# Sorting v of batch 0 from its rows as loaded, and score products behind 128 stationary columns

## The chip, the cores and the metric

The kernel runs on one core of one Trainium2 chip. Its time is the device time of one execution in microseconds, the median of three runs. Beside these runs stands one execution recorded by the hardware profiler; the profile's numbers come from that one. Engines are named as in the profile: PE is the matrix engine's multiplications, PEld its loads of stationary operands, DVE the vector engine, ACT the scalar engine, POOL the third elementwise engine, which also issues most loads from HBM, and SP the queue that issues the rest and the transposing DMAs.

## What is computed

Four batches of eight heads with 768 tokens of 64 elements go through an attention within blocks of 96 tokens, whose keys and values are first mixed between blocks by an 8 by 8 matrix P for each batch and head. Then come two layers of a feed-forward network on all 3072 tokens.

```python
P = sort_net
for _ in range(5):
    P = exp(P - max(P, -1));  P = P / (sum(P, -1) + 1e-9);  P = P / (sum(P, -2) + 1e-9)
k_sorted = einsum('bhij,bhjcd->bhicd', P, k_b)      # k_b: (4, 8, 8 blocks, 96, 64)
v_sorted = einsum('bhij,bhjcd->bhicd', P, v_b)
scores = matmul(q_b, k_sorted^T) / 8                # within a block: 96 x 96
attn = softmax(scores);  x = matmul(attn, v_sorted)
h = x @ w_in                                        # (3072, 512) @ (512, 2048)
out = (max(h, 0) + alpha * min(h, 0)) @ w_out       # (3072, 2048) @ (2048, 512)
```

Inputs and outputs are FP32; the loads turn q, k, v and the weights into BF16.

## The kernel before

The program is first written as a graph of operations (`G.add`: engine, function, estimated duration, the keys that it reads and writes). A table of numbers, `SEQ`, then lists all operations in one order; `arrange` takes each engine's own order from it, and `emit` writes that out with the semaphores that the keys call for. A number in the table is an operation's place in the graph; a letter behind it picks an engine where several may do it. An entry that begins with `i` is a filler: it puts so many matmuls of the identity (`warm`, L1042) into PE's stream, whose results nobody reads. So nothing is scheduled by due times: every engine works through a list that is fixed, and waits where a semaphore says so.

The work is done in 32 groups; group g is block g % 8 of batch g // 8, for all eight heads. `attention(g)` emits for a group:

- `s1` (L752 for batches 1 to 3, L755 for batch 0): eight products of q and sorted k, one for each head, 96 by 96 each, into the two banks of psS (psH for group 1). q is stationary, 96 columns, and k moves. In batch 0 a head uses 64 of the 128 rows of PE, so that two heads can lie on PE at a time.
- the maximum (L761, DVE) over each row of the scores.
- In batch 0 also `s2`: the same products turned (L776: k stationary, `nk` = 112 columns, of which 96 are read later, q moving), and onto them the negated maxima (L767: a stationary operand that repeats one column of `nm` 112 times, and the identity moving). Then one exponent for all heads (L799, ACT) writes ET.
- In the other batches the exponent (L788, ACT) takes the maximum as its bias, and a DMA transposes the result into ET.
- the product with sorted v (L808), its division by the sums (L816, L821), and the transposed copy into xT, directly or by a DMA.

The feed-forward network runs between these steps: `ffn1` (L870, PE; L880, ACT; L884, DVE) and `ffn2` (L910).

v is sorted ahead of its batch in eight units of eight elements of a head each (`prep_v`). For batches 1 to 3 POOL first spreads v into VDz, and PE sorts from there (L709). For batch 0 the rows of v are loaded as they are into VST: a partition holds 48 tokens of 64 elements, `3072` numbers. `conv_v(0, u)` then copies, on POOL, ACT or DVE as the table says, eight elements of all 48 tokens into a corner of the tile hT that is not otherwise in use yet: for each element 48 numbers side by side, and behind them 16 zeros, which one memset on POOL (L480) has written before. `prep_v(0, u)` (L714) takes each of these runs of 64 as a stationary operand, twice, for the upper and the lower 64 partitions of the output, with every second column of the matrix BDK moving. The copies out of PSUM into VS (line L401, where all plain copies have their line) drop nothing but order: v of a block comes to lie with 112 rows, 48 and 48 with zeros between.

```python
o = AP(hT, 8 * u * 64, [[HR, 128], [64, 8], [1, 48]])
i = AP(VST[0], 8 * u, [[3072, 128], [1, 8], [64, 48]])
```

In these access patterns each pair is a step and a count, in elements, the first pair being the partitions; the third number ahead of them is the offset.

Of the kernel before, what the change touches and what calls it, by code (L numbers as in the profile page):

```python
# [7 lines left out]
AP = bass.AP  # L8
ACTF = mybir.ActivationFunctionType
BF16 = mybir.dt.bfloat16  # L10
F32 = mybir.dt.float32
# [22 lines left out]
55 143 56 57 58 26 59 127 60 61 62 21 63 64 126 65 66 22 67 128 68 69 29 70 71 16 72 73 13 74 129 85 86 87 75  # L34
76 77 78 40 79 80 81 37 88 134 82 96 97d 94 91 92 98 38 89 130 12 144 95 90d i2Y 140 93a 83 84 100 i3Y 99d 20
136 101d 102d 105a 103d 154 i3Y 104 106 155 109 114 115 15 145 146 110 111 107d 112 113 i3Y 116 117d 147 108a
118 119d 148 122 123d 137 120 156 121 124 139 132 19 125d 135 233 133 157 i2Y 158 159 149 150 160d i3G 179 180
i1P 41 138 i2P 161 162d 151 152 18 181 30 35 36 34 153d 163 188 182 196 164 165 205 166 167p 197 189 190 191
232 206 183 230 184 207 192 193 185d 198 209 142 199 186 i1Y 231 237 210 141 194 195 221 208 131 187 213 200
211 212 222 244 214 201 223 215 216 248 245 224 249 202d 246 247 203 204d 250 251 217 225 258 218 236 226 262  # L40
263 219 220 234 241 235 227d 266 267 259 260 173 228 229 252 238 276 268 239 253 264 242 269 305 172 288d 170
174 240 280 261 279 286 243 270 315 265 289 290 277 278 271 287 293 294 306 307 272d 273 308 275 291 274 281
292 297 295 342 282d 298 283 309 284 296 301 302 285 316 343 317 310 299 344 300 328 311d 303 304 312 314 313d
320 326 332 32 321d 345 346 327 169p 333 324 329 347 325 353 348d 254 171p 349 334 335 175 354 255 256 350d
323 367 318 395 330 382 331 396 319d 392 336 351 393 383 384 397 394 419 416 420 322 352d 355 356 358d 31 365
398 399 337 366 357 338 408 421 409 359 257 425 417 400 418 426 422 339 428 360d 361 427 423 424 411 449 410
385 340 368 446 429 362 363 439 450 451 455 430 364d 447 448 369 176 458 459 414 443 456 415 386 387 388d 412
452 453 370 454 440 389 401 460 371 438 390d 402 476 488 457 479 413 403 404d 489 405 372 512 177 469 431 406d
432 477 178 441 461 480 444 478 482 442 481 485 433 434d 490 524 491 373 483 472 435 378 377 486 374 436 487
513 380 445 462 375 484 509 463 510 464d 470 379 471 506 507 381 511 465 466d 508 525 514 376 521 522 523 518  # L50
519 520 515 516d 526 527 492 517 474 545 475d 542 168 554 560 391 493 543 546 544 547 468 500 501 494d 555 548
473 561 549 550 502 437 495 496d 562 407 503d 551 552 556 499 577 553 563 578 579 498 504 505 533 528 529 557
558 589 530d 535 534 538 539 571 572 590 583 584 580 341 531 581 625 626 537 536 569 582 586 591 540 587 585
622 570d 541 573 574 575 532 600 576 627 588 623 631 598 624 599 564 632 559 628 629 565 601 634 566d 567 635
602 592 630 603 633 568d 637 636 655 638 639 608 604 605 593 594 595d 610 649 650 640 652 596 653 656 657 609
597 641 642 651 654 664 665 666 661 662 663 606 667 607 658 611 659 687 688 612 668 613 643 684 696 685 660
669 689 686 697 690 691 676 677 682 711 467 680 702 693 694 703 704 683d 695 678 698 692 699 679 713 714 644
645 497 700 670 705 722 723 731 732 810 712 719 720 751 681 733 734 717 817 744 752 646d 812 715 721 724 671
672 725 745 816 718 766 673d 728 767 742 753 726 727 647 729 730 674 706 748 701 757 707 768 618 769 743d 754
708d 758 759 749 750 801 802 755 756 716 746 763 764 747 735 736 760 737d 761 803 765 740 709 762 741 621 789  # L60
777 790 783 784 619 776 786 787 778d 813 785 779 788 836 837 791 792 780 793 775 781 738 804 795 796 782d 811
798 799 797 838 615 814 815d 620 830 770 614 617 818 819 844 845 800 616 771 821 772d 864 831 846 848 874 839
820 648 822 824 823 773 827 805 806 825 794 849 826 832 833 828 807d 829 808 847 872 852 875 865 675 855 873d
834 853 835 850 883 851 854 866 840 841 867 710 876 842d 843 774 877 884 856 857 858 878 879 885 886 898 899
887 859 861 860 912 913 862 880 863 868 869 870d 900 889 924 944 881 882 890 892 891 893 895 925 945 896 894
914 906 926 907 897 908 909 950 910 911 871 946 901 951 927 918 919 920 921 922 923 952 902 903 904d 915 739
932 933 934 935 936 947 948 928 953 970 937 938 939 905 941 942 916d 981 917 982 971 972 943 961 940 958 809
959 973 996 929 1010 930d 931 954 962 997 998 983 960 964 965 963 967 968 1022 955 956d 966 984 969 957 949
999 985 978 979 1023 987 988 980 1042 989 974 975 990 993 1043 1024 1048 976d 994 1044 995 991 992 1004 1005
1049 1007 1008 1050 1011 1012 977 1009 1019 1006 1016 1020 1021 1000 1017 1068 1001 1013 1018 1033 888 1014d  # L70
1034 1030 1031 1079 1080 1069 1002d 1070 1025 1026 1035 1039 1051 1003 1032 1040 1036 1037 1081 1041 1059 1038
1060 1056 1027 1071 1028d 1045 1052 1061 1057 1058 1065 1046 1047 1062 1053 1054d 1066 1082 1067 1085 1063
1064 1086 1055 1087 1072 1076 1015 1073 1100 1074d 1075 1077 1078 1091 1092 1093 1101 1088 1102 1097 1083d
1089 1090 1098 1099 1029 1124 1094 1095 1125 1126 1096 1106 1109 1110 1111 1084 1103 1127 986 1115 1107 1108
1116 1112 1104d 1145 1117 1105 1113 1114 1121 1122 1118 1119 1123 1120 1146 1133 1134 1166 1130 1135 1131 1132
1147 1148 1149 1139 1140 1136 1184 1141 1137 1138 1185 1128d 1151 1142 1152 1143 1153 1172 1157 1144 1154 1155
1156 1186 1173 1158 1174 1159 1160 1161 1162 1150 1163 1164 1165 1167 1168 1169 1187 1129 1188 1170 1189 1175
1176d 1171 1177 1178 1179 1180 1181 1182 1183
# [231 lines left out]
def bass_sinkhorn_attn__then__act_prelu_kernel(  # L310
# [774 lines left out]
```

## Time and profile before

| | |
|---|---|
| time, median of three runs | 235.86 us (235.62 to 236.09) |
| span of the profiled execution | 235.0 us |
| PE busy | 226.5 us (96%) |
| PE's loads of stationary operands busy | 143.5 us (61%) |
| DVE, ACT, POOL busy | 167.1, 156.5, 103.0 us |
| first product of the feed-forward network (L870) | at 29.83 us |
| score products of batch 0 (L755) | 18.1 to 48.8 us |
| score products of the other batches (L752) | 56.0 to 185.9 us |
| units of v of batch 0 on PE (L714) | 19.2 to 24.5 us |

The profile's span runs from the first to the last instruction; what a run takes beyond it, 0.86 us by the median, lies around it. Starts of matmuls are recorded, their ends are modelled: one that takes 40 ns of PE is shown with some 200 ns. So what a block of matmuls costs is read from its start to the start of the next block.

### The profile page before, as it was taken

How to read it: one execution, taken by the hardware profiler on the slowest of the kernel's cores; microseconds unless marked ns; L12 is line 12 of the kernel's file. 1: busy time of each engine (PE TensorE's matmuls, PEld its weight loads, DVE VectorE, ACT ScalarE, POOL GpSimd, SP SyncE). 2: the span in 40 equal slices, each digit the busy share in tenths (PEclk: the TensorE clock that was granted, in tenths of full speed). 3: DMA queues.
4: the chain of work that ended last, by engine and by line, in shares of the span. 5: the costliest groups of instructions: out<-in, count | busy, mean ns of one | idle time of the engine just before them, and what ended most of it. 6: DMA issues, size and time to landing. Idle time of an engine off the chain costs nothing.

```text
span 235.0 us, 6277 instructions
## 1 busy us (share of the span) xinstructions
PE 226.5 (96%) x2528; PEld 143.5 (61%) x2556; DVE 167.1 (71%) x339; ACT 156.5 (67%) x417; POOL 103.0 (44%) x149
## 2 busy tenths in 40 slices
PE   6899999999999999999999999999999999999995
PEld 4366689795566666565566565556565555555653
DVE  5759799999879788576679767567786577544541
ACT  4367565989989778877888767767776665333431
POOL 7999139639249994873959954000000000000000
PEclk9979999999999999999999999999999999999999
DMA  5999999994997799869929995954545423410203
GB/s 71 216 210 193 218 203 183 188 175 75 216 203 115 106 130 187 210 91 228 197 45 152 160 106 137 169 100 78 131 87 138 63 52 106 125 44 1 93 0 134
DMA packets 73389, 31.36 MB, mean 133 GB/s; under 512 B 64512, under 2 KB 68368, under 8 KB 73360
## 3 DMA queue, kind: packets, MB, share of 16 engines
q0 software_dynamic: 24816, 13.63, 43.1%
q1 hardware_dynamic: 48544, 17.33, 36.8%
q8 instruction: 20, 0.33, 0.6%
q14 instruction: 9, 0.07, 0.1%
HBM read 27.28 MB, written 6.29 MB: 143 GB/s over the span
## 4 chain that ended last, share of the span: by engine, by line
PE 92%; DVE 4%; issue 1%; ACT 1%; POOL 1%; POOLq 0%
PE psH L870 35%; PE psYP L910 30%; PE psS L752 4%; PE psS L910 4%; PE psO L808 3%; PE psYP L709 2%; PE psYP L668 2%; PE psYP L1042 2%; PE psS L767 2%; PE psO L843 1%; PE psS L776 1%; PE psS L755 1%; PE psO L714 1%; PE psO L910 1%; PE psYP L870 1%
## 5 line engine op out<-in xcount | busy, mean ns | idle before, releaser
L884 DVE SCALAR_TENSOR_TENSOR hT<-t,omaT,psH 128x384 bf16<-128x384 f32 (+1 forms) x140 | 76.5, 569 | 37.6 <-ACT t L880 36.8
L870 PE MATMUL psH<-xT,w_in_bf 128*128 128x384 bf16 (+1 forms) x560 | 96.7, 310 | 0.6 <-DVE hT L884 0.6
L880 ACT ACTIVATE t<-psH 128x384 f32<-128x384 f32 x126 | 61.1, 494 | 44.4 <-PE psH L870 41.5
L910 PE MATMUL psYP<-w_out_bf,hT 128*128 128x512 bf16 x310 | 79.2, 379 | 1.4
L870 PEld LDWEIGHTS psH<-xT,w_in_bf 128*128 128x128 bf16 x560 | 50.1, 98 | 28.8 <-DVE hT L884 2.1
L910 PEld LDWEIGHTS psYP<-w_out_bf,hT 128*128 128x128 bf16 x336 | 30.8, 98 | 28.2 <-DVE hT L884 0.3
L788 ACT ACTIVATE Esb<-psS,nf 96x96 bf16<-96x96 f32 x192 | 46.3, 346 | 0.9 <-DVE nf L761 0.8
L401 POOL COPY VDz<-VST 64x384 bf16<-64x384 bf16 x40 | 34.6, 865 | 17.3 <-PE psH L870 7.8
L655 POOL COPY KSz<-KS 64x512 bf16<-64x512 bf16 x36 | 21.9, 609 | 17.8 <-DMA KS<-in_k_dram 8.2
L761 DVE TENSOR_REDUCE nf<-psS 96x8 f32<-96x768 f32 x24 | 22.8, 949 | 6.6 <-PE psS L752 6.3
L821 DVE TENSOR_TENSOR xq<-psO,rec 96x512 bf16<-96x512 f32 x30 | 20.5, 684 | 0.7
L431 POOL DMA_DIRECT2D QN<-in_q_dram x24 | 19.9, 846 | 0.7 <-POOL QN L491 0.6
L401 ACT ACTIVATE outstg<-psYP 128x512 f32<-128x512 f32 x15 | 9.0, 601 | 7.7 <-PE psYP L910 7.6
L752 PEld LDWEIGHTS psS<-KT,QTz 128*96 128x96 bf16 x192 | 11.9, 125 | 2.8 <-ACT KT L401 0.2
L808 PEld LDWEIGHTS psO<-VS,ET 112*128 112x128 bf16 x248 | 11.1, 98 | 3.9 <-ACT xT L401 0.2
L808 PE MATMUL psO<-VS,ET 112*128 112x65 bf16 x248 | 12.7, 194 | 0.0
L752 PE MATMUL psS<-KT,QTz 128*96 128x96 bf16 x192 | 12.6, 208 | 0.0
L1042 PE MATMUL psYP<-identb 128*128 128x512 bf16 x39 | 11.6, 436 | 0.8 <-ACT identb L401 0.8
L401 ACT ACTIVATE VS<-psYP 112x512 bf16<-112x512 f32 x16 | 11.0, 690 | 1.9 <-PE psYP L714 1.1
L709 PEld LDWEIGHTS psYP<-BDV,VDz 128*128 128x128 bf16 x192 | 8.4, 98 | 2.7
L401 ACT ACTIVATE KT<-psYP 128x512 bf16<-128x512 f32 x14 | 8.4, 600 | 2.2 <-PE psYP L668 2.1
L816 DVE RECIPROCAL rec<-psO 96x8 f32<-96x8 f32 x31 | 6.2, 200 | 4.8 <-PE psO L808 4.7
(140 smaller groups left out, 208.1 us busy)
## 6 DMA issues: line engine op xcount, KB each, us to landing
out_dram<-outstg SPq DMA_DIRECT2D x23, 256.0 KB, 2.5
KS<-in_k_dram POOLq DMA_DIRECT2D x3, 768.0 KB, 9.7
QN<-in_q_dram POOLq DMA_DIRECT2D x24, 96.0 KB, 4.8
w_in_bf<-in_moe_w_in_dram POOLq DMA_DIRECT2D x4, 512.0 KB, 16.9
w_out_bf<-in_moe_w_out_dram POOLq DMA_DIRECT2D x2, 1024.0 KB, 18.5
VST<-in_v_dram POOLq DMA_DIRECT2D x4, 384.0 KB, 10.6
hT<-in_q_dram POOLq DMA_DIRECT2D x1, 768.0 KB, 7.4
VST<-in_v_dram POOLq DMA_DIRECT2D x1, 768.0 KB, 12.9
```

Of the source, the lines that this page charges most:

```text
L401: return e.activation(o, i, ACTF.Copy) if e is nc.scalar else e.tensor_copy(o, i)
L431: G.add(POOL, lambda e, h=h: e.dma_start(AP(QN, h * 128 + (h // 4) * 64, [[6144, 128], [1024, 6], [1, 64]]), AP(q.tensor, b * HB + h * S * ...
L655: G.add(POOL, lambda e, hp=hp: e.tensor_copy(AP(KSz, hp * 64 * 3072 + u % 3 * 1024 + hp * 64, [[3072, 64], [128, 8], [1, 64]]), AP(KS[n], ...
L752: inst = e.matmul(o, AP(QTz[n], hp * 3072 + h4 * 768 + i * 96, [[6144, 128], [1, 96]]), AP(KT[n], (h4 * 8 + i) * bk, [[ld, 128], [64, 2], ...
L761: G.add(DVE, lambda e: e.tensor_reduce(AP(nx, 0, [[8, 96], [4, 2], [1, 4]]), AP(psX, 0, [[1024, 96], [512, 2], [96, 4], [1, 96]]), AxisLis ...
L788: inst = e.activation(AP(Esb[me], p * 128, [[1024, 96], [64, 2], [1, 48]]), AP(psX, (p // 4) * 512 + (p % 4) * 96, [[1024, 96], [48, 2], [ ...
L808: inst = e.matmul(AP(psZ, hp * 512 + h4 * 68, [[1024, 128], [1, 65]]), AP(ET[me] if far else ET[m], pos(h4, hp) * 96, [[800, nk], [1, 128] ...
L821: return e.tensor_tensor(out=AP(xq[me], 0, [[512, 96], [256, 2], [64, 4], [1, 64]]), in0=AP(psZ, 0, [[1024, 96], [512, 2], [68, 4], [1, 64]]),
L870: inst = e.matmul(AP(pt, poff + x * n, [[1024, 128], [1, n]]), AP(w_in_bf, kt * DFF + (ft + x) * 128, [[KT_TILES * DFF, 128], [1, 128]]), ...
L880: G.add(ACT, lambda e: e.activation(AP(t1[tb], 0, [[384, 128], [1, k * n]]), AP(pt, poff, [[1024, 128], [1, k * n]]), ACTF.Relu, scale=-1. ...
L884: G.add(DVE, lambda e, x=x: e.scalar_tensor_tensor(out=AP(hT, (ft + x) * RING + tok % RING, [[FT_TILES * RING, 128], [1, n]]), in0=AP(t1[t ...
L910: inst = e.matmul(AP(bank[0], bank[1], [[1024, 128], [1, n]]), AP(hT, ft * RING + tok % RING, [[FT_TILES * RING, 128], [1, 128]]), AP(w_ou ...
```

## The change

**v of batch 0.** `load_v(0)` loads the rows of v straight into hT, 3072 numbers in each partition, where VST was the target before. The memset on POOL zeroes the 1024 numbers behind them (L480 before, in one piece now). `conv_v` has no case for batch 0 any more, and its eight operations are gone. `prep_v(0, u)` takes as stationary operand every 64th number from element `8 * u + dd` on: 48 tokens of that element and 16 zeros. It waits for the load of v and for the memset.

**128 columns.** `s1` takes 128 columns of q, the 96 of its block and the 32 behind them; where these would reach beyond what is there, or to tokens that come later, it stays at 96 (`wide`). `s2` takes 128 columns of sorted k (112 for the last head pair of block 7), and the repeated column of maxima stands 128 times. The results land in rows 96 to 127 of the banks, which nothing reads.

```diff
     def load_v(b, prio):
         if b == 0:
-            load_kv(VST, v, "VST", d_v, 9, b, prio)
+            G.add(POOL, lambda e: e.dma_start(AP(hT, 0, [[HR, 128], [1, 3072]]), AP(v.tensor, 0, [[3072, 128], [1, 3072]])),
+                  load_us, w=[("VST", 0)], prio=prio, dma=(d_v[0], 0))
             return
...
-        G.add(POOL, lambda e: e.memset(AP(hT, 48, [[HR, 128], [64, 64], [1, 16]]), 0.0), 900,
+        hz = hT.bitcast(F32)
+        G.add(POOL, lambda e: e.memset(AP(hz, 1536, [[HR // 2, 128], [1, 512]]), 0.0), 500,
               w=["VD0"], prio=-95.5)
...
     def conv_v(b, u, prio):
         vst = [("VST", b % 2)] + [("VST", b % 2, x) for x in range(4)]
-        if b == 0:
-            o = AP(hT, 8 * u * 64, [[HR, 128], [64, 8], [1, 48]])
-            i = AP(VST[0], 8 * u, [[3072, 128], [1, 8], [64, 48]])
-            G.add(ANY, lambda e: copy(e, o, i), {"act": 858, "dve": 540, "pool": 860},
-                  r=vst, w=[("VD", u)], prio=prio)
-            return
...
                     inst = e.matmul(AP(t, th * 64 * row + off + dd * 64, [[row, 64], [1, 64]]),
-                                    AP(hT, (8 * u + dd) * 64, [[HR, 128], [1, 64]]),
+                                    AP(hT, 8 * u + dd, [[HR, 128], [64, 64]]),
                                     AP(BDK, th, [[512, 128], [2, 64]]))
...
-            G.add(PE, f, 374, r=[("VD", u), "VD0", ("BDK", 0)], w=keys, prio=prio)
+            G.add(PE, f, 374, r=[("VST", 0), "VD0", ("BDK", 0)], w=keys, prio=prio)
...
-        qt_keys = [("QTzt", n, t) for t in range(i * 96 // 128, (i * 96 + 95) // 128 + 1)] if far else \
+        def wide(h4, hp):
+            return 96 if far and i == 3 or i == 7 and h4 == 3 and (hp or not far) else 128
+
+        qt_keys = [("QTzt", n, t % 6) for t in range(i * 96 // 128, (i * 96 + wide(0, 0) - 1) // 128 + 1)] if far else \
...
-                    o = AP(psX, (p // 4) * 512 + (p % 4) * 96, [[1024, 96], [1, 96]])
+                    w = wide(h4, hp)
+                    o = AP(psX, (p // 4) * 512 + (p % 4) * 96, [[1024, w], [1, 96]])
                     if far:
-                        inst = e.matmul(o, AP(QTz[n], hp * 3072 + h4 * 768 + i * 96, [[6144, 128], [1, 96]]),
+                        inst = e.matmul(o, AP(QTz[n], hp * 3072 + h4 * 768 + i * 96, [[6144, 128], [1, w]]),
                                         AP(KT[n], (h4 * 8 + i) * bk, [[ld, 128], [64, 2], [1, 48]]))
                     else:
-                        inst = e.matmul(o, AP(QTz[n], hp * 64 * 6144 + h4 * 768 + i * 96, [[6144, 64], [1, 96]]),
+                        inst = e.matmul(o, AP(QTz[n], hp * 64 * 6144 + h4 * 768 + i * 96, [[6144, 64], [1, w]]),
                                         AP(KT[n], hp * 64 * ld + (h4 * 8 + i) * bk, [[ld, 64], [64, 2], [1, 48]]))
...
-            return e.matmul(AP(psX, (p // 4) * 512 + (p % 4) * 96, [[1024, nk], [1, 96]]),
-                            AP(nm[m], p, [[8, 96], [0, nk]]),
+            return e.matmul(AP(psX, (p // 4) * 512 + (p % 4) * 96, [[1024, 128], [1, 96]]),
+                            AP(nm[m], p, [[8, 96], [0, 128]]),
                             AP(identb, 0, [[128, 96], [1, 96]]), start=False, stop=stop, skip_group_check=True)
...
-                    e.matmul(AP(psX, (p // 4) * 512 + (p % 4) * 96, [[1024, nk], [1, 96]]),
-                             AP(KT[n], hp * 64 * ld + (h4 * 8 + i) * bk, [[ld, 64], [1, nk]]),
+                    w = nk if i == 7 and h4 == 3 else 128
+                    e.matmul(AP(psX, (p // 4) * 512 + (p % 4) * 96, [[1024, w], [1, 96]]),
+                             AP(KT[n], hp * 64 * ld + (h4 * 8 + i) * bk, [[ld, 64], [1, w]]),
                              AP(QTz[n], hp * 64 * 6144 + h4 * 768 + i * 96, [[6144, 64], [1, 96]]),
                              start=h4 == 0, stop=False, skip_group_check=True)
...
-    for u in range(8):
-        conv_v(0, u, -45.5)
```

In the table the eight numbers of the copies, 102 to 109, fall out, and every later number is smaller by eight:

```diff
-136 101d 102d 105a 103d 154 i3Y 104 106 155 109 114 115 15 145 146 110 111 107d 112 113 i3Y 116 117d 147 108a
+128 101d 146 i3Y 147 106 107 15 137 138 102 103 104 105 i3Y 108 109d 139 110 111d 140 114 115d 129 112 148 113
```

Apart from the copies the order of every engine is what it was. DVE's list before, from the last copy of sorted k out of PSUM to the factor omaT of the feed-forward network (VST is v as loaded, nm the negated maxima, VS the sorted v):

```order
L401 CAST KT<-psH 128x32x2x8 [waits s_pe]
L401 COPY hT<-VST 128x8x48 [waits d_v0]
L401 COPY hT<-VST 128x8x48
L761 TENSOR_REDUCE nm<-psH 96x8 [waits s_pe]
L761 TENSOR_REDUCE nm<-psS 96x8 [waits s_pe]
L401 COPY hT<-VST 128x8x48
L401 CAST VS<-psO 112x64x8 [waits s_pe] x4
L967 TENSOR_SCALAR omaT<-psYP 128x16 [waits s_pe]
```

and the same place now:

```order
L400 CAST KT<-psH 128x32x2x8 [waits s_pe]
L760 TENSOR_REDUCE nm<-psH 96x8 [waits s_pe]
L760 TENSOR_REDUCE nm<-psS 96x8 [waits s_pe]
L400 CAST VS<-psO 112x64x8 [waits s_pe] x4
L965 TENSOR_SCALAR omaT<-psYP 128x16 [waits s_pe]
```

The three copies have gone from among the maxima and the copies of sorted v; the rest follows in the same order.

PE's list before, from a filler behind the scores of group 1 to the first turned ones (L714 are the units of v, L1042 the fillers, each row with the semaphores that its first instruction waits for):

```order
L1042 MATMUL psYP<-identb 128x512 x3
L714 MATMUL psYP<-BDK,hT 64x64 [waits s_pool]
L714 MATMUL psYP<-BDK,hT 64x64 x15
L755 MATMUL psS<-KT,QTz 96x96 x8
L714 MATMUL psO<-BDK,hT 64x64 [waits s_dve]
L714 MATMUL psO<-BDK,hT 64x64 x15
L714 MATMUL psO<-BDK,hT 64x64 [waits s_dve]
L714 MATMUL psO<-BDK,hT 64x64 x15
L1042 MATMUL psYP<-identb 128x512 x3
L714 MATMUL psO<-BDK,hT 64x64 [waits s_act]
L714 MATMUL psO<-BDK,hT 64x64 x15
L776 MATMUL psS<-QTz,KT 112x96 [waits s_dve]
```

and now:

```order
L1040 MATMUL psYP<-identb 128x512 x3
L709 MATMUL psYP<-BDK,hT 64x64 [waits d_v0,s_pool]
L709 MATMUL psYP<-BDK,hT 64x64 x15
L754 MATMUL psS<-KT,QTz 128x96 x8
L709 MATMUL psO<-BDK,hT 64x64 x32
L1040 MATMUL psYP<-identb 128x512 x3
L709 MATMUL psO<-BDK,hT 64x64 [waits s_act]
L709 MATMUL psO<-BDK,hT 64x64 x15
L776 MATMUL psS<-QTz,KT 128x96 [waits s_dve]
```

No matmul has moved. The first unit of v waits for the load of v (d_v0) and for the memset on POOL, the next two for nothing; the stationary operands of the scores have 128 columns. The lines of before and of now stand against each other thus: L714 and L709, L709 (batches 1 to 3) and L704, L752 and L751, L755 and L754, L767 and L766, L1042 and L1040, L401 and L400.

More of the change, by code (lines that the diff above doesn't have):

```diff
@@ L38 @@
[L38 to L62, printed above, removed]
@@ new lines @@
+619 580 615 623 590 616 591 556 624 551 620 621 557 593 626 558d 559 627 594 584 622 595 625 560d 629 628 647
+630 631 600 596 597 585 586 587d 602 641 642 632 644 588 645 648 649 601 589 633 634 643 646 656 657 658 653
+654 655 598 659 599 650 603 651 679 680 604 660 605 635 676 688 677 652 661 681 678 689 682 683 668 669 674
+703 459 672 694 685 686 695 696 675d 687 670 690 684 691 671 705 706 636 637 489 692 662 697 714 715 723 724
+802 704 711 712 743 673 725 726 709 809 736 744 638d 804 707 713 716 663 664 717 737 808 710 758 665d 720 759
@@ new lines @@
+833 859 702 868 834d 835 766 869 876 848 849 850 870 871 877 878 890 891 879 851 853 852 904 905 854 872 855
+860 861 862d 892 881 916 936 873 874 882 884 883 885 887 917 937 888 886 906 898 918 899 889 900 901 942 902
+903 863 938 893 943 919 910 911 912 913 914 915 944 894 895 896d 907 731 924 925 926 927 928 939 940 920 945
+962 929 930 931 897 933 934 908d 973 909 974 963 964 935 953 932 950 801 951 965 988 921 1002 922d 923 946 954
+989 990 975 952 956 957 955 959 960 1014 947 948d 958 976 961 949 941 991 977 970 971 1015 979 980 972 1034
@@ new lines @@
+981 966 967 982 985 1035 1016 1040 968d 986 1036 987 983 984 996 997 1041 999 1000 1042 1003 1004 969 1001
+1011 998 1008 1012 1013 992 1009 1060 993 1005 1010 1025 880 1006d 1026 1022 1023 1071 1072 1061 994d 1062
+1017 1018 1027 1031 1043 995 1024 1032 1028 1029 1073 1033 1051 1030 1052 1048 1019 1063 1020d 1037 1044 1053
+1049 1050 1057 1038 1039 1054 1045 1046d 1058 1074 1059 1077 1055 1056 1078 1047 1079 1064 1068 1007 1065 1092
+1066d 1067 1069 1070 1083 1084 1085 1093 1080 1094 1089 1075d 1081 1082 1090 1091 1021 1116 1086 1087 1117
```

47 lines of the change are left out of this document (28 added, 19 removed).

## The prediction

> **What bounds the kernel now.** I read the page first, for the engines' shares and the chain that ended last.
>
> ```profile
> span 235.0 us, 6277 instructions
> PE 226.5 (96%) x2528; PEld 143.5 (61%) x2556; DVE 167.1 (71%) x339; ACT 156.5 (67%) x417; POOL 103.0 (44%) x149
> PE 92%; DVE 4%; issue 1%; ACT 1%; POOL 1%; POOLq 0%
> ```
>
> TensorE (PE) is busy for 96% of the span, and 92% of the chain that ended last is PE work. A nanosecond that PE gains or loses should therefore reach the end, unless another engine sets the pace in that stage. Next come the windows, by stage.
>
> ```profile
> core 0: us, PE busy (x) PEld busy (x) DVE busy (x) ACT busy (x) POOL busy (x), PEclk, DMA share, GB/s
> 20.00:30.00 10.00, 9.62 (x215) 6.84 (x212) 7.60 (x19) 7.02 (x17) 4.39 (x6) 1.00 1.12 216
> 30.00:55.00 25.00, 24.89 (x405) 21.16 (x406) 23.53 (x58) 19.29 (x36) 15.90 (x25) 1.00 1.42 175
> ```
>
> The stretch up to 30 us holds the sort of batch 0 and its first groups; 30 to 55 us the rest of batch 0. There DVE is busy for 23.5 of 25 us beside a full PE: there a shorter PE could run into DVE. The granted clock is 1.00 in both.
>
> The profiled execution spans 235.0 us; the three runs have a median of 235.86 us. The 0.86 us between them lies outside the span and I leave it as it is: sums are made on the span and added to the median. What the measurement can tell from no change is 0.2%, here 0.47 us.
>
> **Part one: 128 columns in place of 96 and 112.** No instruction is added; eight groups of batch 0 get wider L755, L776 and L767, 24 groups of the other batches wider L752. What a load costs by its width stands in the groups (mean ns after the busy time):
>
> ```profile
> L752 PEld LDWEIGHTS psS<-KT,QTz 128*96 128x96 bf16 x192 | 11.9, 125 | 2.8 <-ACT KT L401 0.2
> L843 PEld LDWEIGHTS psO<-identb,xq 96*128 96x128 bf16 x60 | 3.7, 97 | 1.1 <-DVE xq L821 0.3
> L714 PEld LDWEIGHTS psO<-BDK,hT 128*64 128x64 bf16 x96 | 1.8, 112 | 0.6 <-ACT VS L401 0.4
> ```
>
> A load of 64 columns takes 112 ns and one of 96 takes 125: it grows with the columns. At 128 columns it takes 97, less than at 64.
>
> What that is worth on PE must be read from starts, since ends are modelled. PE alone, a stretch of batch 0 and a group of batch 1, and then, by line, what one matmul lasts (least, median, most, in ns):
>
> ```profile
> 32.57 0.41 PE L776 MATMUL psS<-QTz,KT 64*112 64x96 bf16 x8
> 32.91 0.61 PE L767 MATMUL psS<-identb,nm 96*112 96x96 bf16 x8
> 33.36 0.83 PE L870 MATMUL psH<-xT,w_in_bf 128*128 128x192 bf16 x8
> 34.02 0.34 PE L843 MATMUL psO<-identb,xq 96*128 96x96 bf16 x4
> 34.19 0.38 PE L1042 MATMUL psYP<-identb 128*128 128x512 bf16 x1
> 34.50 0.38 PE L755 MATMUL psS<-KT,QTz 64*96 64x96 bf16 x8
> 34.81 0.83 PE L870 MATMUL psH<-xT,w_in_bf 128*128 128x192 bf16 x8
> ...
> 56.11 0.52 PE L752 MATMUL psS<-KT,QTz 128*96 128x96 bf16 x8
> 56.47 0.81 PE L870 MATMUL psH<-xT,w_in_bf 128*128 128x384 bf16 x4
> ...
> L776 PE MATMUL psS<-QTz,KT x56: 212/212/247, 21.6 to 50.7; 64*112 64x96 bf16 x56
> L755 PE MATMUL psS<-KT,QTz x56: 205/205/240, 19.6 to 48.8; 64*96 64x96 bf16 x56
> ```
>
> L767: eight in 33.36 - 32.91 = 0.45 us, 56 ns each. L843 has the same 96 moving columns behind 128 stationary ones: four in 0.17 us, 43 ns each. So L767 falls to about 8 x 44 = 0.35, a gain of 0.10 us a group.
> L776 works in pairs on the two halves of the rows; its eight take 0.34 us. One matmul lasts 0.212, so starts are (0.41 - 0.212)/7 = 28 ns apart, 57 a pair; a pair can't go below the 44 of one moving operand, so 22 each: 7 x 6 = 0.04 us a group.
> L755, likewise: (0.38 - 0.205)/7 = 25, to 22: 0.02 us a group.
> L752: eight in 0.36 us, 45 ns each, which is what L843 takes with a fast load. The moving operand sets it, and the load lies beneath it. Gain: nothing, in 24 groups.
> Sum: 8 x (0.10 + 0.04 + 0.02) = 1.3 us at most. Bounds: if loads of half the rows stay slow at 128 columns, L776 gets 16 columns dearer (as from L755 to L776, 3 ns each) and L755 twice that, some 0.6 us in all, and 0.2 us is left of L767's 0.8. And where DVE sets the pace from 30 us on, only the three groups before it count: 0.5 us. [...]
> I take 0.9, between 0.5 and 1.3: PE and the chain of score, maximum, exponent through the banks psS both get shorter, but DVE has only 1.5 us free there.
>
> **Part two: v of batch 0 as loaded.** Eight copies go: three on POOL, three on DVE, two on ACT. What stood behind them, in order of time:
>
> ```profile
> 17.09 3.24 POOL L401 COPY hT<-VST 128x384 bf16<-128x384 bf16 x3
> ...
> 17.98 1.62 DVE L401 COPY hT<-VST 128x384 bf16<-128x384 bf16 x2
> 19.52 0.94 DVE L761 TENSOR_REDUCE nm<-psH 96x8 bf16<-96x768 f32 x1
> ...
> 21.61 0.28 PEld L776 LDWEIGHTS psS<-QTz,KT 64*112 64x112 bf16 x8
> ...
> 32.95 0.61 POOL L655 COPY KSz<-KS 64x512 bf16<-64x512 bf16 x1 [8.21 <-DMA KS<-in_k_dram]
> ```
>
> The first maximum, and the one behind it, can start 1 us earlier, but L776, which reads them, stands in PE's order behind four of the v units and a filler, and PE reaches it at 21.6 either way. On POOL the q loads of batch 1 are issued some 3 us earlier, and then POOL waits 8.2 us for k of batch 1, as before: nothing moves behind 32.95. The first v unit now waits for the DMA of v itself; POOL's first copy of it ran at 17.1, two us before PE gets there. PE's own waits here are few:
>
> ```profile
> PEld psO L714 <- ACT VS L401: 0.4, 1, 0.4
> PEld psYP L808 <- DVE omaT L967: 0.7, 1, 0.7
> ```
>
> The first is for a bank to be emptied and mostly lies under a filler of L1042; the second is behind the last v unit, whose copy out stays. So the copies' going is worth 0.1 us at most. They hid behind PE's fillers; I book nothing.
>
> The added cost is in the loads. The same 128 matmuls (L714) take 64 columns that lay side by side; now each column lies 128 bytes behind the last. The trace has no load with such a step. PE's pace there (its blocks in order of time, what one of L714 lasts, and a piece of the chain of waits for scale), and what such a step costs the three engines that made the copies, with a like one in order beside each:
>
> ```profile
> 19.86 0.69 PE L714 MATMUL psO<-BDK,hT 128*64 128x64 bf16 x32
> 20.49 0.82 PE L1042 MATMUL psYP<-identb 128*128 128x512 bf16 x3
> ...
> 29.83 0.83 PE L870 MATMUL psH<-xT,w_in_bf 128*128 128x192 bf16 x8
> ...
> L714 PE MATMUL psO<-BDK,hT x96: 192/196/217, 19.9 to 24.5; 128*64 128x64 bf16 x96
> ...
> 54.76 0.86 PE psYP L910 x4
> ...
> L401 DVE COPY hT<-VST x3: 508/598/1187, 18.0 to 21.3; 128x384 bf16<-128x384 bf16 x3
> L401 ACT ACTIVATE hT<-VST x2: 853/855/857, 17.7 to 21.4; 128x384 bf16<-128x384 bf16 x2
> ...
> L401 DVE COPY xT<-psO 128x384 bf16<-128x384 bf16 x9 | 3.2, 353 | 0.5 <-PE psO L843 0.4
> L880 ACT ACTIVATE t<-psH 128x384 f32<-128x384 f32 x126 | 61.1, 494 | 44.4 <-PE psH L870 41.5 <-DVE hT L884 1.8
> L401 POOL COPY VDz<-VST 64x384 bf16<-64x384 bf16 x40 | 34.6, 865 | 17.3 <-PE psH L870 7.8 <-PE psYP L709 5.6 <-DMA VST<-in_v_dram 1.9
> L655 POOL COPY KSz<-KS 64x512 bf16<-64x512 bf16 x36 | 21.9, 609 | 17.8 <-DMA KS<-in_k_dram 8.2 <-PE psYP L668 7.7
> ```
>
> Thirty-two L714 take 0.63 us, 20 ns each with the block's start, starts (0.69 - 0.196)/31 = 16 apart inside. A column of a moving operand takes 0.42 ns (L910's four of 512 in 0.86 us), so 64 take 27: the two halves of the output run side by side, and a load has some 32 ns before it is late. It has no slack to lose more than a few ns in.
> The step's price per element: ACT (855 - 494)/384 = 0.94 ns, POOL 865/384 - 609/512 = 1.06 ns, DVE at its best (508 - 353)/384 = 0.40 ns. The least it can be is 0. For 64 columns: 0, 26 (DVE) or 60 ns (ACT) a load; with two halves side by side 0, 13 or 30 ns a matmul; times 128: 0, 1.65 or 3.85 us, on PE, in a stage without slack, ahead of all the rest. If the halves' loads queue, the last two double.
> I take DVE's, 1.65 us: PE's column of 0.42 ns is nearest to DVE's pace, and 0.40 more makes one column in two clocks of it.
> [...]
>
> **Sum.** 235.86 + 1.65 - 0.9 = 236.6 us. Its own range: 235.86 + 1.65 - 1.3 = 236.2, up to 237.5 with half of ACT's excess.
>
> **The rivals.**
> *Loads with a step cost PE nothing.* Then part one is all: 235.86 - 0.9 = 235.0, from 234.6 to 235.4. For it: a copy made to put columns side by side may have been made only for the 16 zero columns at the end of each 64. Against: ACT, POOL and DVE all pay. It decides if L714's starts stay 16 ns apart. Chance 0.32.
> *They cost what ACT pays.* 235.86 + 3.85 - 0.9 = 238.8, from 237.5 up to 242.7 where the two halves' loads also queue. For it: two engines of three agree at about 1 ns. [...] Chance 0.22.
> *Little of either.* The step is free or cheap, and DVE at 94% eats what PE gains after 30 us: within 0.47 us of 235.86. Against: PE's starts there stand close. Chance 0.08.
> The forecast keeps 0.38.
>
> **How the numbers follow.** Faster: the first rival, 0.32, and none of the others. Same: 0.08 and a little of the forecast's low end (236.2 to 236.33), 0.10. Slower: the rest, 0.58. The range takes in the free step, the forecast and the lower part of ACT's price: 234.6 to 239.0. What is left out is the upper half of that last case, about 0.1, and as much for what I have not thought of.
>
> **What would show it.** In the changed profile: L714 (there L709) starts apart by 28 to 30 ns in the x32 block (16: the first rival; 45 or more: the second), and the block 0.4 us longer. L767 (there L766) at 44 ns each, its load at 97 ns. L752 (there L751) at 45 still. DVE's first maxima about 1 us earlier, to no effect. PE's first L870, now at 29.83 us, later by 1.65 - 0.5 = 1.15 us, since three groups of part one lie ahead of it. If that first L870 comes earlier, the forecast is wrong in sign.

## The result and the profile after

The changed kernel takes 242.66 us (median of 4 runs, 241.67 to 243.01), the kernel before 235.90 us beside it (4 runs, 235.62 to 236.09). The ratio is 1.0258 [1.0228, 1.0288]: slower by 2.6%. The forecast was 236.6 us, with a range up to 239.0. The sign was right; the size was not. Of the rivals' ranges only the far end of the dear one, 242.7, reaches it.

The page of the profiled execution (243.01 us outside, span 241.1): its span, PE's busy time, the granted clock in 40 slices of 6 us.

```profile
span 241.1 us, 6267 instructions
PE 233.2 (97%) x2528; PEld 147.3 (61%) x2556; DVE 165.4 (69%) x336; ACT 154.7 (64%) x415; POOL 99.0 (41%) x146
PEclk9997569999999999999999999999999999999999
```

PE is busy for 6.7 us more in a span that is 6.1 us longer, so what was lost was lost on PE. (Between span and time lie 1.9 us here, and 1.7 to 2.0 in every run that has both on record. The 0.86 us given for the kernel before sets the span of one execution against the median of others.) The clock row shows something new: 7, 5 and 6 tenths in the slices from 18 to 36 us. PE's timeline of that stretch (start, length to the end of the last one, line, instruction, count):

```profile
17.87 1.19 PE L709 MATMUL psYP<-BDK,hT 128*64 128x64 bf16 x16
18.99 0.34 PE L754 MATMUL psS<-KT,QTz 64*128 64x96 bf16 x8
19.26 2.20 PE L709 MATMUL psO<-BDK,hT 128*64 128x64 bf16 x32
21.39 1.46 PE L1040 MATMUL psYP<-identb 128*128 128x512 bf16 x3
22.79 1.18 PE L709 MATMUL psO<-BDK,hT 128*64 128x64 bf16 x16
23.89 0.50 PE L776 MATMUL psS<-QTz,KT 64*128 64x96 bf16 x8
...
25.08 2.02 PE L709 MATMUL psO<-BDK,hT 128*64 128x64 bf16 x32
26.91 1.18 PE L709 MATMUL psYP<-BDK,hT 128*64 128x64 bf16 x16
28.02 0.50 PE L776 MATMUL psH<-QTz,KT 64*128 64x96 bf16 x8
...
29.21 1.22 PE L709 MATMUL psO<-BDK,hT 128*64 128x64 bf16 x16
30.35 0.28 PE L962 MATMUL psYP<-identf,alphaR 16*128 16x16 f32 x1
...
35.50 0.34 PE L776 MATMUL psS<-QTz,KT 64*128 64x96 bf16 x8
...
36.62 0.83 PE L870 MATMUL psH<-xT,w_in_bf 128*128 128x192 bf16 x8
```

Two things are to be seen. The v block of 32 (L709) runs from 19.26 to 21.39, 2.13 us where L714 took 0.63. All v blocks together, each from its start to the next one's: 1.12 + 2.13 + 1.10 + 2.94 + 1.14 = 8.43 us, against 2.62 in the kernel before: 5.8 us more. And what stands between them got longer without having been changed: three fillers L1040 take 1.46 us (0.82 at full clock), eight L776 0.50 (0.34 at 35.50). The windows give the clock:

```profile
core 0: us, PE busy (x) PEld busy (x) DVE busy (x) ACT busy (x) POOL busy (x), PEclk, DMA share, GB/s
17.00:21.00 4.00, 4.00 (x63) 3.26 (x59) 1.91 (x2) 1.22 (x2) 3.45 (x5) 1.00 1.08 188
21.00:28.00 7.00, 7.00 (x91) 5.43 (x89) 2.09 (x3) 1.66 (x3) 0.00 (x0) 0.50 1.14 216
28.00:35.00 7.00, 7.00 (x67) 4.25 (x66) 2.50 (x6) 3.21 (x10) 1.69 (x3) 0.52 1.12 206
```

From 21 to 35 us PE runs at half its clock, although its records show it busy without a gap. The first L870 starts at 36.62, not 29.83 us, and the rest follows as before. How long the half clock lasts differs from run to run: the mean granted clock is 0.972 in two of the four runs, the profiled one among them (243.01 and 242.97 us), and 0.986 in the other two (242.34 and 241.67).

The profiled execution of before has a dip of its own, from about 14 to 17 us. One row of its windows:

```profile
14.00:15.00 1.00, 1.00 (x47) 1.00 (x44) 0.31 (x1) 0.54 (x3) 1.00 (x3) 0.50 1.01 209
```

It makes PE come to the first v unit at 19.18 us, where the changed kernel comes at 17.87. Most other runs of before, at a mean clock of 0.999 or 1.000, have no such dip. So stages are compared from the first v unit on.

### The profile page after: what moved, and what is told of

It is laid out like the page before. It is cut to its first block, busy times and chain, and to the rows that moved or that the text cites. A ratio compares the mean times of both kernels' runs of the same rounds, so it can differ in the third digit from the quotient of the medians.

```text
span 241.1 us, 6267 instructions
## 1 busy us (share of the span) xinstructions
PE 233.2 (97%) x2528; PEld 147.3 (61%) x2556; DVE 165.4 (69%) x336; ACT 154.7 (64%) x415; POOL 99.0 (41%) x146
## 4 chain that ended last, share of the span: by engine, by line
PE 91%; DVE 3%; ACT 2%; issue 1%; POOL 1%; POOLq 0%
PE psH L870 34%; PE psYP L910 29%; PE psS L910 4%; PE psS L751 3%; PE psO L808 3%; PE psO L709 3%; PE psYP L704 2%; PE psYP L669 2%; PE psYP L1040 2%; PE psS L766 1%; PE psO L843 1%; PE psYP L709 1%; PE psS L776 1%; PE psS L754 1%; ACT KT L400 1%
## 5 line engine op out<-in xcount | busy, mean ns | idle before, releaser
L870 PE MATMUL psH<-xT,w_in_bf 128*128 128x384 bf16 (+1 forms) x560 | 96.8, 310 | 0.6 <-DVE hT L884 0.6
L870 PEld LDWEIGHTS psH<-xT,w_in_bf 128*128 128x128 bf16 x560 | 50.0, 98 | 29.0 <-DVE hT L884 2.1
L400 POOL COPY VDz<-VST 64x384 bf16<-64x384 bf16 x40 | 34.4, 861 | 17.3 <-DMA VST<-in_v_dram 9.8
L400 ACT ACTIVATE VS<-psYP 112x512 bf16<-112x512 f32 x16 | 11.0, 690 | 5.3 <-PE psYP L709 4.5
L400 ACT ACTIVATE outstg<-psYP 128x512 f32<-128x512 f32 x15 | 9.0, 601 | 7.7 <-PE psYP L910 7.5
L1040 PE MATMUL psYP<-identb 128*128 128x512 bf16 x39 | 13.0, 476 | 0.8 <-ACT identb L400 0.8
L751 PEld LDWEIGHTS psS<-KT,QTz 128*128 128x128 bf16 (+1 forms) x192 | 10.7, 102 | 3.2 <-ACT KT L400 0.2
L751 PE MATMUL psS<-KT,QTz 128*128 128x96 bf16 (+1 forms) x192 | 12.2, 207 | 0.0
L704 PEld LDWEIGHTS psYP<-BDV,VDz 128*128 128x128 bf16 x192 | 8.3, 98 | 2.8 <-ACT t L880 0.2
L400 ACT ACTIVATE KT<-psYP 128x512 bf16<-128x512 f32 x14 | 8.4, 600 | 2.2 <-PE psYP L669 2.0
```

Of the source, the lines that this page charges most:

```text
L400: return e.activation(o, i, ACTF.Copy) if e is nc.scalar else e.tensor_copy(o, i)
L751: inst = e.matmul(o, AP(QTz[n], hp * 3072 + h4 * 768 + i * 96, [[6144, 128], [1, w]]), AP(KT[n], (h4 * 8 + i) * bk, [[ld, 128], [64, 2], [ ...
L870: inst = e.matmul(AP(pt, poff + x * n, [[1024, 128], [1, n]]), AP(w_in_bf, kt * DFF + (ft + x) * 128, [[KT_TILES * DFF, 128], [1, 128]]), ...
```

## The experiments

The theory at this point: the stepped loads cost about 45 ns a matmul (5.8 us / 128), and they also bring the half clock. The rivals: the copies' removal or a new wait is to blame; part one is; the cost hangs on banks or on the length that a load spans.

**Part one alone.** The kernel before with the 128 columns only:

```diff
-  o = AP(psX, ..., [[1024, 96], [1, 96]])
+  w = wide(h4, hp)
+  o = AP(psX, ..., [[1024, w], [1, 96]])
...
-  AP(nm[m], p, [[8, 96], [0, nk]]),
+  AP(nm[m], p, [[8, 96], [0, 128]]),
```

> The kernel before with part one alone (128 stationary columns; v still copied, its columns side by side). Theory A (all of the loss comes from the stepped loads of v, and part one is a gain): 234.7 us, 1.2 below before, L766's kind at 44 ns a matmul, the granted clock as before. Rival B (the wider operands themselves lose, in clock or in pace): 236 us or more.

Measured: 235.20 us (12 runs, 234.57 to 235.60), ratio 0.9947 [0.9927, 0.9968] to the kernel before. Its timeline, and its groups of weight loads by shape (busy us, mean ns):

```profile
28.18 0.34 PE L781 MATMUL psS<-QTz,KT 64*128 64x96 bf16 x8
28.45 0.52 PE L771 MATMUL psS<-identb,nm 96*128 96x96 bf16 x8
28.90 0.26 PE L587 MATMUL psYP<-Pb,selk 32*128 32x64 bf16 x3
...
L756 PEld LDWEIGHTS psS<-KT,QTz 128*128 128x128 bf16 x165 | 9.0, 98 | 2.9 <-ACT KT L401 0.2
L771 PEld LDWEIGHTS psS<-identb,nm 96*128 96x128 bf16 x56 | 2.6, 98 | 0.5
L781 PEld LDWEIGHTS psS<-QTz,KT 64*128 64x128 bf16 x54 | 1.3, 94 | 0.7 <-issue 0.2 <-DVE nm L765 0.2 <-DVE xq L826 0.2
```

L781 (was L776) goes from 0.34 to 0.27 us a group and L771 (was L767) by about 0.10 (four of eight from 0.45 to 0.35, three with a block of v or L587 behind them from 0.54 to 0.45, one only to 0.42). The load of 64 rows takes 94 ns at 128 columns, as fast as one of 96 or 128 rows. This kernel is faster than both others, than the one before by 0.5%.

**The v rows alone.** The changed kernel with 96 and 112 columns as before.

> The changed kernel with part one undone (96 and 112 stationary columns again), v sorted from its rows as loaded. Theory A: 243.5 us, about 1 above the changed kernel, the units of v at 66 to 70 ns a matmul and the granted clock at a half from about 21 to 35 us. Rival B: 236 us.

Measured: 244.58 us (4 runs, 243.27 to 245.83), 1.0359 [1.0317, 1.0400]: 1.9 us above the changed kernel, where I had expected 1. So part one gains here too, and the whole loss lies in part two.

**All of the change except the step.** The stationary columns side by side (v is then not sorted right):

```diff
-  AP(hT, 8 * u + dd, [[HR, 128], [64, 64]]),
+  AP(hT, (8 * u + dd) * 48, [[HR, 128], [1, 64]]),
```

> The changed kernel with the stationary operands of v taken as 64 numbers side by side (so v is not sorted rightly), with no copies, the same waits and the same order. Theory A (the step between columns is the cause): units of v at 16 ns a matmul, no long stretch at half clock, 234.7 us as with part one alone. Rival C (the cause is what else part two changed: the load into hT, the waits, the missing copies): 242 us still.

Measured: 235.12 us (7 runs, 234.79 to 235.34), 0.9957 [0.9943, 0.9971], the same as part one alone. PE's timeline:

```profile
18.90 0.70 PE L709 MATMUL psO<-BDK,hT 128*64 128x64 bf16 x32
...
28.41 0.83 PE L870 MATMUL psH<-xT,w_in_bf 128*128 128x192 bf16 x8
```

The v blocks are at their old pace, and the copies' going is worth nothing that can be measured (0.08 us between the medians). The step alone, 64 in place of 1, costs 242.66 - 235.12 = 7.5 us. (The two stood beside different series of the kernel before, with medians of 235.90 and 236.22; by the ratios it is 3.0%, or 7.1 us.)

**What in the step costs.** Three variants, each run once, with each unit of v in another form (v not sorted right). In the first the step is 1, 2, 4, 8, 16, 32 and 64 elements, and 64 once more with one half of the output's eight matmuls in a row, then the other's.

> The changed kernel with another step between the stationary columns in each unit of v, in the order in which PE comes to them: 1, 2, 4, 8, 16, 32, 64 numbers of two bytes, and 64 again with the loads for the two halves of the output in groups of four instead of in turn (v is not sorted rightly). Line theory (a load pays for each new line of 16 bytes): 16 ns a matmul at steps 1 to 4, 66 at 8 to 64. Bank theory (only the step of 128 bytes meets the same bank each time): 16 ns up to 32, 66 at 64 alone. Span theory (the farther, the dearer): rising from 1 to 64. The unit in groups: 66 ns still if the two halves' loads go one after the other, 130 in each group if they had gone side by side.

The second, whose edits read like this for each unit:

```diff
+  if u == 2:
+      for th, d in ((dd // 4, dd % 4 * 2), (dd // 4, dd % 4 * 2 + 1)):
...
+  elif u == 1:
+      ... e.matmul(AP(t, off + dd * 64, [[row, 128], [1, 64]]), AP(hT, 8 * u + dd, [[HR, 128], [8, 128]]), ...)
...
+  elif u == 4:
+      ... e.matmul(..., AP(hT, 8 * u + dd, [[HR, 128], [1, 64]]), AP(hT, 8 * u + dd, [[HR, 128], [64, 64]]))
...
```

> One look: each unit of v in another form, so the output is not the reference's. In PE's order: unit 2 has step 64 with one half's eight loads in a row, then the other's; unit 0 has 128 stationary columns side by side, unit 1 128 columns of step 8, unit 3 128 columns of step 32; unit 4 has columns side by side but a moving operand of step 64; unit 6 has 64 columns of step 6, unit 5 of step 3, unit 7 of step 1. Starts of one unit's sixteen. If a load costs 0.9 ns for every 16-byte line that it touches: unit 6 (48 lines) 43 ns, unit 5 (24 lines) 22 ns, unit 7 16 ns, unit 3 (128 lines) 115 ns, unit 1 (128 lines) 115 ns, unit 0 27 to 30 ns. If each column that isn't next to the last one costs the same whatever its line, units 6 and 5 are both near 58 ns. If loads of the two halves overlap, unit 2 takes 86 ns or more a matmul at full clock; if they queue, 58 ns there too. If a stepped moving operand pays as well, unit 4 is near 58 ns, else 16.

The third took up what the second left open:

> One look: each unit of v in another form, so the output is not the reference's. With one half's eight loads in a row, a matmul of step 64 took 87 ns, against 58 to 62 where the halves take turns. Either a load alone costs 58 and the half's own matmul (27 ns) can't run beneath it, so 85; or a load alone costs 87 and two halves' loads overlap by a third. In PE's order, with one half's loads in a row where it says so. Unit 2, columns side by side in a row: 27 ns if the load lies beneath the matmul, some 43 if they go in turn. Unit 0, step 64 in a row with up to 256 columns moved (87 ns in the mean): 145 ns if in turn, 90 to 105 if beneath. Unit 1, step 64 in a row: 87 again. Unit 4, step 4 in a row: 56 if in turn, 43 if beneath. Unit 3, 128 columns of step 4, 64 lines in all: 30 ns, half of the 60 to 62 of step 8 and 32. Unit 6, step 64 with the halves taking turns: 58 to 62.

PE's timelines of the three variants, a piece of each; the rows with x4 and x3 are narrow windows at the end of a row:

```profile
19.17 0.45 PE L710 MATMUL psYP<-BDK,hT 128*64 128x64 bf16 x16
...
20.11 0.66 PE L716 MATMUL psO<-BDK,hT 128*64 128x64 bf16 x16
...
21.46 1.13 PE L719 MATMUL psO<-BDK,hT 128*64 128x64 bf16 x16
...
25.20 1.18 PE L728 MATMUL psYP<-BDK,hT 128*64 128x64 bf16 x16
```
```profile
19.47 1.59 PE L710 MATMUL psYP<-BDK,hT 128*64 128x64 bf16 x16
...
20.45 0.61 PE L710 MATMUL psYP<-BDK,hT 128*64 128x64 bf16 x4
...
21.75 1.13 PE L716 MATMUL psO<-BDK,hT 128*128 128x64 bf16 x16
...
25.16 1.14 PE L722 MATMUL psO<-hT 128*64 128x64 bf16 x16
26.11 0.83 PE L725 MATMUL psO<-BDK,hT 128*64 128x64 bf16 x16
```
```profile
18.67 0.59 PE L710 MATMUL psYP<-BDK,hT 128*64 128x64 bf16 x16
...
19.01 0.26 PE L710 MATMUL psYP<-BDK,hT 128*64 128x64 bf16 x3
...
19.47 1.47 PE L713 MATMUL psO<-BDK,hT 128*64 128x256 bf16 x13
...
19.69 0.51 PE L713 MATMUL psO<-BDK,hT 128*64 128x256 bf16 x3
...
20.67 0.30 PE L716 MATMUL psO<-BDK,hT 128*64 128x64 bf16 x1
...
20.95 0.24 PE L713 MATMUL psO<-BDK,hT 128*64 128x64 bf16 x1
...
22.86 0.72 PE L719 MATMUL psO<-BDK,hT 128*128 128x64 bf16 x16
...
24.83 0.29 PE L722 MATMUL psO<-BDK,hT 128*64 128x64 bf16 x2
...
24.95 0.23 PE L722 MATMUL psO<-BDK,hT 128*64 128x64 bf16 x1
```

Starts are taken as in the prediction: a block less the mean length of one matmul (0.19 to 0.30 us by its group), over the count less one. "Lines" counts the pieces of 16 bytes, 8 elements, that the operand touches in a partition; at a step of 8 each column has its own, and from there on the cost no longer grows (56 ns at 8, 59 at 64). "In turns" means that the loads for the two halves of the output alternate; the number is the mean over the block, so two matmuls, one on each half, take twice that. "One half alone" is read from single starts in the trace, where one half's loads stand in a row and the other half has none at the time: the x4 row of the second variant holds 20.455, 20.565, 20.677 and 20.787 us.

| variant | stationary operand of one matmul | lines touched | ns between starts |
|---|---|---|---|
| 1 | 64 columns, step 1; step 2, halves in turns | 8; 16 | 17; 17 |
| 1 | 64 columns, step 4, halves in turns | 32 | 29 |
| 1 | 64 columns, step 8; 16; 32; 64, halves in turns | 64 | 56; 58; 58; 59 |
| 2 | 64 columns, step 3; step 6, halves in turns | 24; 48 | 22; 39 |
| 1, 2, 3 | 64 columns, step 64, one half alone | 64 | 110 |
| 3 | 64 columns, step 4, one half alone | 32 | 60 |
| 3 | 64 columns, step 1, one half alone | 8 | 31 |
| 3 | 64 columns, step 64, one half alone, 256 columns moved | 64 | 116 |
| 2 | 128 columns, step 1; step 8; step 32 | 16; 128; 128 | 30; 60; 62 |
| 3 | 128 columns, step 4 | 64 | 35 |
| 2 | 64 columns side by side, moving operand of step 64 | 64 moved | 56 |

What follows:
- With 64 columns and the halves in turns the cost goes by these lines of 16 bytes, about 0.9 ns each from 24 of them on. Steps of 8 to 64 elements cost nearly the same, 56 to 59 ns, where the bank theory had 16 up to a step of 32 and the span theory a rise all the way; 48 lines cost 39 ns and 24 cost 22, so it isn't a flat price for any column that is not next to the last one. My line theory had a step of 4 as free; its 32 lines cost 29 ns against 17.
- A load of 64 lines takes 110 ns by itself, 1.7 a line; one of 32 lines takes 60; one in order lies within 31. With 256 columns moved (107 ns at 0.42 a column) a stepped load and its matmul take 116 together, not 110 + 107. So here a load lay beneath the matmul before it.
- The two halves' loads ran side by side. With the halves in turns PE's records come in pairs: at a step of 8 they start at 21.715 and 21.720, 21.833 and 21.837, 21.950 and 21.955 us. A pair of loads takes 118 ns where one alone takes 110; at a step of 4 the pair takes 62 and one alone 60. So a line costs a load 1.7 to 1.9 ns, and two halves in turns 0.8 to 0.9 a matmul.
- The mean over a whole block with one half in a row, then the other, is misleading: 87 ns ((1.59 - 0.284)/15). Half 1's row starts while half 0's is still under way (its first matmul starts 6 ns behind one of the other half, at 19.939 against 19.933 us), so some of the sixteen overlap and some don't. Neither way in which I had explained the 87 ns for the third variant holds: a load alone costs neither 58 nor 87.
- A moving operand with the step of 64 paid too: 56 ns where 64 columns in order take 17 with the halves in turns.
- My expectation of 115 ns for 128 stepped columns was wrong: 60, or 0.47 a line. A load of twice the columns took about half as long as one of 64 alone (110). Why, no run here shows.

**More columns moved behind the same loads.** Does the half clock come from the loads, or from how little the array moves behind them? Each stepped matmul moves its columns up to four times over, with the same result:

```diff
+  r = min(4, 8 - dd)
-  inst = e.matmul(AP(..., [[row, 64], [1, 64]]),
+  inst = e.matmul(AP(..., [[row, 64], [1, 64 * r]]),
...
-  AP(BDK, th, [[512, 128], [2, 64]]))
+  AP(BDK, th, [[512, 128], [0, r], [2, 64]]))
```

> Each stepped matmul of v moves its 64 columns up to four times over (256 columns, two halves side by side: 256 x 0.42 = 107 ns a pair, while a pair's two stepped loads take 2 x 58 = 116), so the stepped loads still set the pace and the output is the same. Theory: PE's clock halves after the change because slow loads leave the array with few columns to move in the stretch from 18 us on. Then the granted clock stays near 1.00 from 18 to 35 us, the v block of 32 still takes 2.0 to 2.2 us, the three L1040 behind it 0.82 and not 1.46 us, and the time falls by the 2.5 us lost at half clock, to about 240.2 us. Rival: the loads themselves, or where the stage stands in time, halve the clock. Then the clock is 0.50 from 22 to 34 us as in the changed kernel, and the time 242.7 us or more.

Measured: 241.25 us (4 runs, 240.77 to 242.06), 1.0211 [1.0168, 1.0253]. Its windows and a piece of PE's timeline:

```profile
21.00:28.00 7.00, 7.00 (x103) 6.22 (x105) 2.36 (x4) 2.54 (x4) 0.00 (x0) 1.00 1.14 215
28.00:35.00 7.00, 6.62 (x99) 4.60 (x98) 3.78 (x12) 3.21 (x10) 1.69 (x3) 1.00 1.12 205
...
20.81 2.21 PE L710 MATMUL psO<-BDK,hT 128*64 128x256 bf16 x32
22.96 0.82 PE L1041 MATMUL psYP<-identb 128*128 128x512 bf16 x3
```

The loads are as slow (2.15 us for 32), and the clock stays at 1.00. That held in the runs without a profile as well: their mean granted clock is 1.000 three times, against 0.986, 0.986 and 0.972 in the changed kernel's. So here it is the columns moved, not the loads as such. Moving 3.25 times the columns (the mean over the eight elements of a unit) made the kernel no slower, and by the medians 1.4 us faster; the two ratios' intervals overlap, so the clock is what this run settles, and not the microseconds. I had expected 240.2; the v blocks got 0.4 us longer (8.86 us in all) and the profiled execution has the early dip.

**Half of the units stepped**, every second one in PE's order (v not sorted right).

```diff
-  AP(hT, 8 * u + dd, [[HR, 128], [64, 64]]),
+  AP(hT, 8 * u + dd, [[HR, 128], [64, 64]]) if u in (1, 2, 4, 5) else
+  AP(hT, (8 * u + dd) * 48, [[HR, 128], [1, 64]]),
```

> Only four of the eight units of v, every second one in PE's order, are read with a step of 64 elements; the other four are read side by side, so they are not sorted right. Theory one, a price per load: 64 of 128 matmuls cost about 46 ns more each, 2.9 us over the kernel with side-by-side columns (235.1 us), so 238.1 us, with the clock at 1.00 throughout. Theory two, the clock: the halved clock comes as soon as the stretch from 18 us on holds some stepped loads; then there is a stretch at 0.50 to 0.65 behind them, and the time is 239.5 us or more. If both halves of the loss were one thing of the clock alone, the stepped blocks would be short (0.4 us for 16) while the clock is 1.00.

Measured: 237.46 us (10 runs, 237.03 to 238.00), 1.0046 [1.0027, 1.0066]; the mean granted clock is 1.000 in all ten.

```profile
17.87 1.17 PE L709 MATMUL psYP<-BDK,hT 128*64 128x64 bf16 x16
18.98 0.34 PE L755 MATMUL psS<-KT,QTz 64*128 64x96 bf16 x8
19.25 1.40 PE L709 MATMUL psO<-BDK,hT 128*64 128x64 bf16 x32
20.58 0.82 PE L1041 MATMUL psYP<-identb 128*128 128x512 bf16 x3
21.33 0.44 PE L709 MATMUL psO<-BDK,hT 128*64 128x64 bf16 x16
```

The first unit is stepped and takes 1.11 us, the one at 21.33 is not and takes 0.38. The v blocks come to 5.56 us, 2.94 over the 2.62 of before, 46 ns for each of 64 matmuls; the time is 2.3 us above that with columns side by side (expected 3.0). So the price is per load, at full clock too, and the half clock is a second loss, which four units of stepped loads in turns with four others did not bring. The first variant above has that loss too. From 21.46 to 26.32 us four units that touch 64 lines a load stand there, with only one group of scores among them, and from 27 us on the clock is at half:

```profile
27.00:28.00 1.00, 1.00 (x15) 0.95 (x13) 0.00 (x0) 0.92 (x2) 0.00 (x0) 0.50 1.24 242
```

## Why the prediction was wrong

**The step that failed: the price of a stepped load.** I took DVE's 0.40 ns an element, 26 ns a load, and let the two halves' loads run side by side, 13 ns a matmul and 1.65 us. The overlap was right: a pair takes 118 ns, one alone 110. The price was too low by a factor of three. A load of 64 lines takes 110 ns and one in order lies within 31, so the step costs at least 79 ns a load or 1.2 a column, more than ACT's 0.94 or POOL's 1.06, which I had as the upper end. In the changed kernel starts are 61 ns apart ((2.20 - 0.301)/31, with 301 ns for one L709), where I had named 28 to 30 for the forecast and 45 or more for the second rival. That is 5.8 us on 128 matmuls where I booked 1.65.

The second rival, ACT's price, was nearest, and still too cheap: 3.85 us with the loads side by side. Its far end, 235.86 + 7.7 - 0.9 = 242.7 us, is the measured time, but that is luck. It supposed that the halves' loads queue, which they don't, and had no change of clock in it. I had left it out of the range all the same.

The reason given for DVE, that one column of 0.42 ns is nearest to DVE's pace, was a likeness of numbers and no mechanism; two of the three engines in the trace paid about 1 ns, and nothing in the trace said that PE was better. The 0.40 itself came from the fastest of three copies (508 ns; the median of 598 gives 0.64), set beside a copy out of PSUM. A slip besides: half of ACT's excess over DVE's, 1.1 us, on top of 236.6 gives 237.7 us and not 237.5; nothing hangs on it.

The forecast priced the step by the element, whatever its length. The runs show a cost that grows with the step up to 16 bytes: 8 elements of 2 bytes are where it stops growing (56 ns a matmul at a step of 8, 59 at 64), a step of 2 costs what a step of 1 does (17 ns), and one of 4 costs 29.

**The step that was missing: the clock.** No rival had the granted clock in it. The account from the medians: 235.90 + 5.8 (loads) - 1.2 (part one) = 240.5, measured 242.66; the 2.2 us left are about what the half clock costs. The rows of the profiled execution say 2.8: from the start of the x32 block to the first L870 it takes 36.62 - 19.26 = 17.36 us, with columns side by side 28.41 - 18.90 = 9.51, and of these 7.85 us the v blocks are 5.0 (7.3 against 2.3). The rest is in fillers, scores and maxima. Another way: the three undipped runs with more columns moved take 240.77 to 241.33 us, with v blocks that are 0.4 us dearer, so some 240.7 without the dip, and 2.0 for it. And the changed kernel's two runs with the longer dip take 1.0 us more than the two with one about half as long. The loads themselves lose nothing at half clock (48 in 2.94 us, 61 ns each). So PE was busy in every record (7.00 of 7.00 us from 21 to 28 us) and had a granted clock of 0.50 all the same, with few columns moved behind slow loads. Why it fell at 21 us and not before, and why it came back after 13 to 14 us, no run shows.

**What held.** Part one: booked 0.9 us, at most 1.3; measured 0.53% [0.32%, 0.73%], or 1.25 us. L767 fell by the 0.10 a group that was worked out (in one group by 0.03), L776 by 0.05 to 0.07 where I had 0.04, L755 by 0.03 where I had 0.02. That loads of 64 rows get faster at 128 columns too, on which L776's and L755's shares rested, no row of before shows; with part one alone they take 94 ns, where before they took 126 at 112 columns (L776) and 120 at 96 (L755). DVE did not eat the gain. Over the eight groups the rows come to 0.7 + 0.5 + 0.2 = 1.4 us, of which 1.25 arrive at the end. L751 takes 0.34 us for eight against 0.36, next to nothing, as booked.

**The copies.** Booked at nothing, and worth nothing: 235.12 against 235.20 us. DVE's first maximum did move, from 19.52 to 17.22 us, and PE reads it at 23.9 at the earliest. POOL's waits are where they were:

```profile
POOL KSz L656 <- DMA KS<-in_k_dram: 12.0, 1, 12.0
DVE VS L400 <- PE psO L709: 8.0, 4, 3.7
```

POOL waits longer for the same k, which lands when it did (KSz starts at 32.78, before at 32.95). DVE now waits 8.0 us for v's units, which costs nothing by itself.

**The first L870.** Predicted later by 1.15 us; later by 6.8, and by 8.1 counted from the first v unit (18.75 us against 10.65), since the profiled execution of before had come to that unit 1.3 us later. The loss is complete there, and behind it the kernel gains back 0.7, the rest of part one: the span grew by 6.1.

## What to carry to other kernels

Before an operand is read in place with a step, count the pieces of 16 bytes that one load touches, and take the time of a load in order only if they lie within what the matmul hides: here about 1.8 ns a piece for a load of 64 columns (110 to 118 ns for 64), two halves' loads side by side, so 0.9 a matmul. Copies that run beneath other work were the cheaper way to put columns side by side: their going was worth 0.08 us by the medians, and the step cost 7.5. Where PE is busy but moves few columns, look at the granted clock before and after, since the loss may spread to neighbours that nobody changed: here three fillers took 1.46 us at a clock of 0.50, and 0.82 at 1.00. Of the three kernels, the one with the wider stationary operands and the copies kept is the one to use: 0.9947 [0.9927, 0.9968].

## What the runs showed of the hardware

- A stationary operand of 64 columns of two bytes cost by the pieces of 16 bytes (lines) it touched: 17 ns a matmul at 8 and 16 of them, 22 at 24, 29 at 32, 39 at 48, 56 to 59 at 64 (halves in turns; first and second variant). A moving operand of step 64 took 56 (second variant).
- Loads for the two halves of the output columns ran side by side: a pair of 64 lines each took 118 ns, one alone 110; at 32 lines 62 and 60.
- A load of 128 stepped columns took 60 to 62 ns at 128 lines, about half of one of 64 columns alone (110 ns). By the line, too, the wide load was cheaper (0.47 ns against 1.7).
- The load's price did not change with the clock: 61 ns a matmul at 0.50 as at 1.00 in the changed kernel.
- Loads of 64 rows took 94 ns at 128 columns with part one alone, and 126 at 112 columns in the kernel before.
- The two halves of the output columns went on by themselves: in the third variant the next unit's first matmul on one half starts at 20.67 us, while the last of the unit before it on the other half starts at 20.95.
- The granted clock fell to 0.50 for 13 to 14 us with PE's records at 7.00 of 7.00 us busy, and stayed at 1.00 when the same loads had up to four times the columns moved behind them. How few columns for how long bring it down was not found: four stepped units in turns with four others did not, in ten runs (mean clock 1.000). Three close together came before the fall in the changed kernel (17.87 to 21.39 us), and four in the one run of the first variant (0.50 from 27 us on).
